# Attention with a gated, routed feed-forward: VectorE's side jobs placed at another point of the block

## The chip, the cores and the metric

The kernel runs on one core of a Trainium2 chip. The metric is the device time of one launch in microseconds (us). Times are medians of several runs; one further execution was taken by the hardware profiler, and its trace is what the profile shows. Engines: PE is TensorE (matmuls), DVE is VectorE, ACT is ScalarE, POOL is GpSimd, SP is SyncE, which here only issues DMAs. Each engine works through its own instructions strictly in the order in which they are written; across engines only semaphores order them.

## What is computed

Cut to what matters (2048 tokens of width 640, 32 heads of width 192, the last 512 rows of the key and value caches, feed-forward width 1536):

```python
xn = layernorm(x)                                  # [2048, 640]
q  = xn @ wq                                       # 32 heads x 192
p  = softmax(q @ k.T * 192**-0.5)                  # per head, 512 keys
s  = concat(p @ v) @ wo                            # [2048, 640]
r   = xn @ w_r                                     # one number per token
idx = the 2 tokens with the largest r              # the routed rows
y   = (silu(xn[idx] @ w_gate) * (xn[idx] @ w_up)) @ w_down * sigmoid(r[idx])
b   = xn with y added to the 2 rows idx
out = x + s * silu(b)
```

Nearly all work is the attention `s`. The routed feed-forward touches two rows only, but needs `r` of all 2048 tokens, a search for the two largest, a gather of these two rows, their own layernorm, and three small matrix products.

## The kernel before

The whole order of work is written out by hand; no scheduler changes it.

**Blocks.** Work goes in 128 numbered blocks. A block b handles, for one pair of heads, 256 query tokens as two halves a = 0, 1 of 128 tokens; two blocks (even, odd) make a step of 512 tokens, 16 blocks a group of four heads over all tokens. From block 12 to block 125 each block emits the tokens of the string `BLOCK = "A S0 M0 W m E0 B S1 M1 P E1 l"`:

- A and B (L340): the two halves of the query projection of the next step on PE, ten matmuls each. In even blocks they have 512 columns, in odd blocks 256, so A and B are long in even blocks and short in odd ones. B is told to wait for the row maximum before it. After B, ACT moves the result to `qT` (L352).
- S0, S1 (L367): scores of one half, six matmuls into one of two PSUM buffers. M0, M1 (L372): DVE's row maximum of these scores, `nm`. E0, E1 (L377): ACT's exponentials, which need `nm`; after E1, SP issues the DMA that transposes them (`pT`, L383).
- W (L447): output projection `wo` of an item six blocks back, 24 matmuls into two PSUM banks; DVE adds both to the accumulator `s_acc` (L468, L470). In this text that is "wo's eviction".
- P: the product with V for block b-2 (L406), 32 matmuls, the second half of them after everything in the list `bg[b]`. Then DVE takes two reciprocals (`rl`, L413), ACT scales one PSUM bank in two instructions (`o_sb`, L420) and DVE the other (`o_sb`, L417): "P V's eviction". SP transposes `o_sb` by DMA (L423). The PSUM banks of P and W come from one pool of two, so W of the next block needs the banks that P V's eviction clears.
- m and l are the two side places: lists of small jobs, by block number.

**Side jobs.** `mid[b]` runs at m, so on DVE behind wo's eviction and ahead of M1. `bg[b]` runs inside P, so on DVE behind M1 and ahead of `rl`. `loads[b]` runs at l, at the end of the block, and holds DMA issues of SP and ACT and copies of POOL: `wo_double` (L151) copies a loaded piece of `wo` to the other 64 partitions, `k_order` (L121) permutes a loaded piece of K. POOL starts these copies when the load has landed.

The routed rows' jobs on DVE: `m_r(n)` (L648, blocks 12 to 27, one each) multiplies a tile of 128 tokens of `xn` by `w_r` and sums; `m_round`, `m_rows` (28) turn the sums; `m_top` (29) finds the two best of each tile, and POOL issues two DMAs that write them to DRAM and read them back to all partitions (L681, L683); `m_sel` (32, m) and `m_tok` (32, inside P) choose the two tokens; `m_own` (33) makes the indices, and POOL issues the gather of the two rows (L717); `m_gather` gives seven pieces (36 to 39, in turn at m and inside P): the mask `oh` (L734), statistics (L186), Newton steps for the root in four pieces (L207 to L222), and the normalised rows `xsel` (L751); `m_ffn(fb)` (blocks 41, 49, 57, inside P) does the gate and up products, ACT's tanh (L772) and two DVE products (L773, L774), and in the block behind turns the result on PE (L778); `m_sig` (60, inside P) makes the sigmoid. From block 71 POOL adds `y` to each tile (L828, L831, L832), and from block 76 on, in every even block at m, DVE forms the gate of one tile (L841); the change leaves these as they are.

Of the kernel before, what the change touches and what calls it, by code (L numbers as in the profile page):

```python
# [13 lines left out]
BF16 = mybir.dt.bfloat16  # L14
# [7 lines left out]
def kernel(ctx, tc, A_x, A_k_cache, A_v_cache, A_wq, A_wo, B_x, B_w_r, B_w_gate, B_w_up, B_w_down, out):  # L22
    nc = tc.nc
    P = 128
# [7 lines left out]
    NTB = S // P  # L32
# [41 lines left out]
    def f_tile(shape, dtype, name, kind="q"):  # L74
        return banks[kind].tile(shape, dtype, name=name, tag="f")
# [107 lines left out]
    def ln_stats(src, mv_ap, parts=P):  # L183
        stats = small.tile([P, nsub, nc.vector.BN_STATS_DIM], FP32, name="stats")
        for c in range(nsub):
            nc.vector.bn_stats(out=stats[0:parts, c, :], in_=src[:, c * sub:(c + 1) * sub])  # L186
        nc.vector.bn_aggr(out=mv_ap, in_=stats[0:parts])
# [8 lines left out]
    def ln_nmr(mean_ap, rstd_ap, nmr_ap):  # L196
        nc.vector.scalar_tensor_tensor(out=nmr_ap, in0=mean_ap, scalar=-1.0, in1=rstd_ap, op0=ALU.mult, op1=ALU.mult)

    def rsqrt_newton(var_ap, out_ap, parts, n):

        T = {}

        def one():
            T["v"] = small.tile([P, 4], FP32, name="nw_v")[0:parts, 0:n]
            T["a"] = small.tile([P, 4], FP32, name="nw_a")[0:parts, 0:n]
            T["i"] = small.tile([P, 4], I32, name="nw_i")[0:parts, 0:n]
            nc.vector.tensor_scalar(out=T["v"], in0=var_ap, scalar1=EPS, scalar2=None, op0=ALU.add)  # L207

        def two():
            nc.vector.tensor_scalar(out=T["i"], in0=T["v"].bitcast(I32), scalar1=1, scalar2=None, op0=ALU.arith_shift_right)  # L210

        def three():
            nc.vector.tensor_scalar(out=out_ap.bitcast(I32), in0=T["i"], scalar1=-1.0, scalar2=float(0x5f3759df), op0=ALU.mult, op1=ALU.add)

        def s1():
            nc.vector.scalar_tensor_tensor(out=T["a"], in0=out_ap, scalar=-0.5, in1=out_ap, op0=ALU.mult, op1=ALU.mult)

        def s2():
            nc.vector.tensor_tensor(out=T["a"], in0=T["a"], in1=T["v"], op=ALU.mult)

        def s3():
            nc.vector.scalar_tensor_tensor(out=out_ap, in0=T["a"], scalar=1.5, in1=out_ap, op0=ALU.add, op1=ALU.mult)  # L222
        return [one, two, three] + [s1, s2, s3] * 3
# [256 lines left out]

    bg = defaultdict(list)
    mid = defaultdict(list)
    loads = defaultdict(list)

    def ln_parts(t5):
# [35 lines left out]
    copies = {"a": nc.scalar.copy, "v": nc.vector.tensor_copy}  # L521

    def flush(k):
        for f in mid.pop(k, []) + loads.pop(k, []) + bg.pop(k, []):
            f()

    def first(token):
# [96 lines left out]
    M = {}  # L624
# [20 lines left out]
    def m_r(n):  # L645
        def f():
            junk = M["s"].tile([P, D], BF16, name="junk", tag="t1")
            nc.vector.scalar_tensor_tensor(out=junk, in0=xn[:, n, :], scalar=1.0, in1=M["wr"], op0=ALU.mult, op1=ALU.mult,  # L648
                                           accum_out=M["r"][:, n:n + 1])
        return f  # L650
# [70 lines left out]
    def m_ffn_piece(fb, q):  # L721
        def f():
            if q == 0:
                M["wgu"] = M["w"].tile([P, 2, DC, 512], BF16, name="wgu", tag="w")
            w, dc = divmod(q, DC)
            src = (B_w_gate, B_w_up)[w].rearrange("(c p) f -> p c f", p=P)
            nc.scalar.dma_start(out=M["wgu"][:, w, dc, :], in_=src[:, dc, fb * 512:(fb + 1) * 512])
        return f

    def m_gather():  # L730

        def mask():
            for j in range(2):
                nc.vector.tensor_scalar(out=M["oh"][:, :, j], in0=M["iota"], scalar1=M["best"][:, 1, j:j + 1], scalar2=0.5,  # L734
                                        op0=ALU.is_equal, op1=ALU.mult)

        def begin():
            M["mv2"] = M["s"].tile([2, 2], FP32, name="mv2")
            M["rs2"] = M["s"].tile([2, 2], FP32, name="rs2")
            ln_stats(M["xg"], M["mv2"], parts=2)  # L740
            M["nw"] = rsqrt_newton(M["mv2"][:, 1:2], M["rs2"][:, 0:1], 2, 1)

        def newton(q):
            for f in M["nw"][3 * q:3 * q + 3]:
                f()

        def apply():
            mv2, rs2 = M["mv2"], M["rs2"]
            ln_nmr(mv2[:, 0:1], rs2[:, 0:1], rs2[:, 1:2])
            M["xsel"] = M["s"].tile([2, D], BF16, name="xsel", tag="t3")  # L750
            nc.vector.tensor_scalar(out=M["xsel"], in0=M["xg"], scalar1=rs2[:, 0:1], scalar2=rs2[:, 1:2], op0=ALU.mult, op1=ALU.add)  # L751
        return [mask, begin] + [lambda q=q: newton(q) for q in range(4)] + [apply]
# [8 lines left out]
    def m_ffn(fb):  # L761

        def mul():
            gu = f_tile([P, 2, P], FP32, "gu_ps")
            for dc in range(DC):
                for c in range(4):
                    nc.tensor.matmul(gu[32 * c:32 * c + 32], lhsT=M["xsT"][:, dc, :], rhs=M["wgu"][:, :, dc, c * P:(c + 1) * P],
                                     start=(dc == 0), stop=(dc == DC - 1), skip_group_check=True)
            th = M["s"].tile([P, 3, P], FP32, name="th", tag="t2")
            M["h"] = M["s"].tile([P, P], BF16, name="h")  # L770
            nc.vector.tensor_copy(out=th[:, 0:2], in_=gu)
            nc.scalar.activation(out=th[:, 2], in_=th[:, 0], func=ACT.Tanh, scale=0.5)  # L772
            nc.vector.scalar_tensor_tensor(out=th[:, 2], in0=th[:, 2], scalar=1.0, in1=th[:, 0], op0=ALU.add, op1=ALU.mult)  # L773
            nc.vector.scalar_tensor_tensor(out=M["h"], in0=th[:, 2], scalar=0.5, in1=th[:, 1], op0=ALU.mult, op1=ALU.mult)  # L774

        def turn():
            h_ps = f_tile([P, P], BF16, "h_ps")
            nc.tensor.transpose(out=h_ps, in_=M["h"], identity=ident)  # L778
            nc.vector.tensor_copy(out=M["hT"][:, fb * 4:(fb + 1) * 4, :].rearrange("p c t -> p (c t)"), in_=h_ps)
        return mul, turn  # L780

    def m_wd_piece(h, q):
        def f():
            if q == 0:
                M["wd"] = M["w"].tile([P, FC, HD], BF16, name="wd", tag="w")
            nc.scalar.dma_start(out=M["wd"][:, 2 * q:2 * q + 2, :],
                              in_=B_w_down.rearrange("(c p) d -> p c d", p=P)[:, 2 * q:2 * q + 2, h * HD:(h + 1) * HD])
        return f
# [53 lines left out]
        return a, b  # L842

    bg[11].append(m_open)
    for n in range(NTB):
        mid[12 + n].append(m_r(n))
    mid[28].append(m_round)
    bg[28].append(m_rows)
    mid[29].append(m_top)
    mid[32].append(m_sel)  # L850
    bg[32].append(m_tok)
    mid[33].append(m_own)
    for q, it in enumerate(m_gather()):
        (mid, bg)[q % 2][36 + q // 2].append(it)
    bg[40].append(m_xsT)
    pieces = {0: (33, (2, 2, 2, 1, 2, 1)), 1: (42, (2, 2, 2, 2, 2)), 2: (49, (2, 2, 2, 1, 2, 1))}
    for fb, km in enumerate((41, 49, 57)):
        k0, counts = pieces[fb]
        at = [k0 + h for h, n in enumerate(counts) for _ in range(n)]
        for q, a in enumerate(at):  # L860
            loads[a].append(m_ffn_piece(fb, q))
        mul, turn = m_ffn(fb)
        bg[km].append(mul)
        bg[km + 1].append(turn)
    for h in range(2):
        for q, a in enumerate((57, 58, 58, 59, 59, 60)):
            loads[a + 5 * h].append(m_wd_piece(h, q))
    bg[60].append(m_sig)
    bg[62].append(m_down(0))
    bg[68].append(m_down(1))  # L870
    bg[69].append(m_sum)
    for n in range(NTB):
        bg[71 + 2 * n].append(m_add(n))
        a, b = m_gate(n)
# [34 lines left out]
    for b in range(HEAD, NB - 2):  # L909
        for token in BLOCK:  # L910
            if token in "AB":
                if b // 2 + 1 < NS:
                    q_phase(b // 2 + 1, ((0, 1), (2,))[b % 2], "AB".index(token))
            elif token[0] == "S":
                scores(b, int(token[1]))
            elif token[0] == "M":
                row_max(b, int(token[1]))
            elif token[0] == "E":
                exps(b, int(token[1]))
            elif token == "W":  # L920
                w_item(b - LAG)
            elif token == "P":
                def between():
                    for f in bg.pop(b, []):
                        f()
                o_item(b - 2, "va", between)
            else:
                for f in {"m": mid, "l": loads}[token].pop(b, []):
                    f()

    def last(token):
# [27 lines left out]
    """.split()  # L959
    for token in LAST:  # L960
        last(token)
    assert not bg and not mid and not loads


# [28 lines left out]
```

## Time and profile before

| what | value |
|---|---|
| median of 3 runs | 808.72 us (808.2 to 810.61) |
| the profiled execution | 807.77 us, span in the trace 806.0 us |
| PE busy | 783.0 us, 97% of the span |
| DVE, ACT, POOL busy | 591.0, 529.3, 310.1 us |
| granted TensorE clock | 1.0 |
| `m_r` on DVE (L648) | 16 instructions, 17.5 us |
| copies of POOL (L151; L121) | 32, 59.3 us; 30, 25.1 us |

A timeline row gives the start in the span, the duration, engine, line, operation, out<-in with shapes, how many instructions were merged into it, and in brackets the idle time of the engine before it with the instruction that ended it. PE's matmuls overlap in the pipeline, so a PE row that starts late need not show all of the lateness as idle time.

### The profile page before, as it was taken

What the parts mean: (1) busy time and instruction counts of PE and PEld (TensorE: products, weight loads), DVE (VectorE), ACT (ScalarE), POOL (GpSimd) and SP (SyncE); (2) the same over time, 40 slices, a digit from 0 to 9 for tenths busy, and PEclk for the clock granted to TensorE, in tenths of its full rate; (3) what the DMA queues carried; (4) which work ended last, traced back from release to release, by engine and by line L of the source; (5) the groups of instructions that cost most, each with busy time, mean ns of one, the idle gap of its engine ahead of it and who ended that gap; (6) DMA issues with size and microseconds to landing.
All of it is one profiled execution on the core that took longest, in us unless ns stands there. A gap on an engine that the chain in (4) does not pass through costs nothing.

```text
span 806.0 us, 26621 instructions
## 1 busy us (share of the span) xinstructions
PE 783.0 (97%) x11354; PEld 579.1 (72%) x11354; DVE 591.0 (73%) x1086; ACT 529.3 (66%) x964; POOL 310.1 (38%) x244
## 2 busy tenths in 40 slices
PE   8799899999999999999999999999999999999997
PEld 4366577777777777777777777777777777777775
DVE  7686588778778667777666667777777777767775
ACT  5677566665666666666666667677776776666662
POOL 1312120011110100101011699959997412564865
PEclk9999999999999999999999999999999999999999
DMA  7998998798999999999998999989898899999992
GB/s 193 188 175 161 199 169 154 152 189 143 191 199 160 181 208 200 196 188 191 200 211 159 171 192 166 182 137 184 173 186 149 153 190 163 209 190 163 178 181 84
DMA packets 445111, 142.29 MB, mean 177 GB/s; under 512 B 412228, under 2 KB 444488, under 8 KB 444992
## 3 DMA queue, kind: packets, MB, share of 16 engines
q1 hardware_dynamic: 435216, 131.18, 93.1%
q10 hardware_dynamic: 8816, 6.88, 3.3%
q0 software_dynamic: 960, 2.52, 1.0%
q8 instruction: 89, 1.46, 0.8%
q14 instruction: 30, 0.25, 0.1%
HBM read 39.98 MB, written 2.62 MB: 53 GB/s over the span
## 4 chain that ended last, share of the span: by engine, by line
PE 85%; DVE 5%; DMA 4%; ACT 3%; issue 2%; POOL 0%; SPq 0%; ACTq 0%; DVEq 0%; POOLq 0%
PE w L447 24%; PE q_ps L340 21%; PE o_ps L406 18%; PE s L367 18%; DVE nm L372 2%; DMA pT<-pexp 2%; PE q_ps L309 2%; ACT o_sb L420 1%; ACT pexp L377 1%; PE warm_ps L163 1%; DMA xnT<-xn 1%; DMA oT<-o_sb 1%; DMA wo_g<-in_A_wo_dram 1%; DMA v_sb<-in_A_v_cache_dram 0%; ACT qT L315 0%
## 5 line engine op out<-in xcount | busy, mean ns | idle before, releaser
L372 DVE TENSOR_REDUCE nm<-s 128x2 f32<-128x1024 f32 x256 | 313.0, 1223 | 135.6 <-PE s L367 131.0
L377 ACT ACTIVATE pexp<-s,nm 128x512 bf16<-128x512 f32 x512 | 323.3, 688 | 90.3 <-DVE nm L372 53.9
L447 PE MATMUL w<-wo_g,oT 64*128 64x320 bf16 x3072 | 231.1, 296 | 4.8 <-ACT o_sb L420 4.5
L340 PE MATMUL q_ps<-xnT,wq_g 64*128 64x512 bf16 (+1 forms) x2340 | 232.4, 323 | 3.2 <-DMA xnT<-xn 1.5
L447 PEld LDWEIGHTS <-oT 64*128 64x128 bf16 x3072 | 171.8, 94 | 62.9 <-issue 7.5
L367 PE MATMUL s<-kT,qT 64*128 64x512 bf16 x1536 | 211.7, 376 | 5.0 <-ACT pexp L377 3.9
L406 PEld LDWEIGHTS <-pT 64*128 64x128 bf16 x4096 | 179.1, 94 | 27.9 <-issue 2.0
L406 PE MATMUL o_ps<-v_sb,pT 64*128 64x193 bf16 x4096 | 197.2, 243 | 0.0
L420 ACT ACTIVATE o_sb<-o_ps,rl 128x192 bf16<-128x192 f32 x256 | 93.6, 417 | 145.7 <-DVE rl L413 140.6
L340 PEld LDWEIGHTS <-wq_g 64*128 64x128 bf16 x2340 | 127.4, 99 | 48.3 <-issue 2.6
L151 POOL COPY wo_g<-wo_g 64x1920 bf16<-64x1920 bf16 x32 | 59.3, 1858 | 222.3 <-DMA wo_g<-in_A_wo_dram 202.1
L367 PEld LDWEIGHTS <-qT 64*128 64x128 bf16 x1536 | 85.4, 94 | 59.8 <-issue 6.4
L470 DVE TENSOR_TENSOR s_acc<-s_acc,w 128x320 f32<-128x320 f32 x192 | 85.0, 484 | 35.4 <-PE w L447 35.4
L352 ACT ACTIVATE qT<-q_ps 128x1024 bf16<-128x1024 f32 x114 | 92.4, 810 | 7.7 <-PE q_ps L340 2.8
L121 POOL COPY k_perm<-k_raw 128x768 bf16<-128x768 bf16 x30 | 25.1, 854 | 143.3 <-DMA k_raw<-in_A_k_cache_dram 111.9
L417 DVE TENSOR_TENSOR o_sb<-o_ps,rl 128x384 bf16<-128x384 f32 x128 | 71.4, 558 | 4.6 <-DVE rl L413 0.2
L831 POOL TENSOR_SCALAR yh<-y_bc,oh 128x640 bf16<-128x640 bf16 x32 | 61.7, 1929 | 3.3 <-DMA y_bc<-y_d 1.7
L832 POOL TENSOR_TENSOR xn<-xn,yh 128x640 bf16<-128x640 bf16 x32 | 44.6, 1395 | 2.7
L413 DVE RECIPROCAL rl<-o_ps 128x2 f32<-128x2 f32 x256 | 30.0, 159 | 14.4 <-PE o_ps L406 8.2
L894 POOL TENSOR_TENSOR s_acc<-s_acc,x_fin 128x640 f32<-128x640 f32 x16 | 22.4, 1397 | 31.3 <-DMA x_fin<-in_A_x_dram 30.8
L828 POOL TENSOR_SCALAR xn<-xn 128x640 bf16<-128x640 bf16 x16 | 29.4, 1838 | 0.8
L478 POOL TENSOR_TENSOR fin_o<-fin_t,s_acc 128x640 bf16<-128x640 f32 x12 | 18.5, 1540 | 17.7 <-DVE fin_t L473 11.1
(138 smaller groups left out, 262.4 us busy)
## 6 DMA issues: line engine op xcount, KB each, us to landing
wo_g<-in_A_wo_dram SPq DMA_DIRECT2D x32, 240.0 KB, 4.3
k_raw<-in_A_k_cache_dram SPq DMA_DIRECT2D x32, 192.0 KB, 3.6
v_sb<-in_A_v_cache_dram SPq DMA_DIRECT2D x32, 192.0 KB, 4.3
wq_g<-in_A_wq_dram SPq DMA_DIRECT2D x14, 288.0 KB, 4.1
wq_g<-in_A_wq_dram SPq DMA_DIRECT2D x14, 192.0 KB, 3.7
x_fin<-in_A_x_dram SPq DMA_DIRECT2D x16, 160.0 KB, 3.6
pT<-pexp SPq DMA_TRANSPOSE x130, 4.9
oT<-o_sb SPq DMA_TRANSPOSE x126, 3.4
```

The source lines that it names most:

```text
L151: nc.gpsimd.tensor_copy(out=grp[g][("wo", pr)][half(1), cs, :], in_=grp[g][("wo", pr)][half(0), cs, :])
L340: mm = nc.tensor.matmul(q_ps[k][:, 0:n] if type(q_ps) is list else q_ps[:, k, 0:n], lhsT=wq[half(r), dc, c:2 * Dh:3], rhs=xnT[half(r), tok ...
L352: nc.scalar.activation(out=out, in_=q_ps[:, :, 0:n], func=ACT.Copy, scale=scale)
L367: nc.tensor.matmul(s_of[b, a][:, r, :], lhsT=qT_of[i][half(r), c, u * P:(u + 1) * P], rhs=grp[g][("kT", pr)][half(r), :, c, :], start=(c = ...
L372: rm = nc.vector.tensor_reduce(out=nm_of[b, a], in_=s_of[b, a], axis=AX.X, op=ALU.max, negate=True)
L377: nc.scalar.activation(out=p_ring[:, b % 2, a, :, hh, :].rearrange("p (x j) e -> p x j e", x=2), in_=s_of[b, a][:, hh, :].rearrange("p (j ...
L406: nc.tensor.matmul(o_of[b][r][:, a, 0:Dh + 1], lhsT=pT_ring[half(r), b % RP, a, k, :], rhs=v_ring[half(r), (g * PAIRS + pr) % RV, k, 0:Dh ...
L417: nc.vector.tensor_tensor(out=o_sb, in0=src, in1=rl[:, r].unsqueeze(2).unsqueeze(3).to_broadcast([P, 2, 3, HK]), op=ALU.mult)
L420: nc.scalar.activation(out=o_sb[:, a], in_=src[:, a], func=ACT.Copy, scale=rl[:, r, a:a + 1])
L447: nc.tensor.matmul(w_ps[r][:, 0:HD], lhsT=oT_ring[half(r), bs[pr] % RT, c, :], rhs=grp[g][("wo", pr)][half(r), c, cs], start=(pr == 0 and ...
L470: nc.vector.tensor_tensor(out=acc, in0=acc, in1=src, op=ALU.add)
L831: nc.gpsimd.tensor_scalar(out=yh, in0=M["y_bc"][:, j, :], scalar1=M["oh"][:, n, j:j + 1], scalar2=None, op0=ALU.mult)
```

## The change

A third list, `end[b]`, runs at l ahead of `loads[b]`: on DVE behind P V's eviction, and so ahead of M0 of the next block. A helper, `spot(b)`, chooses `mid` for even blocks and `end` for odd ones. `m_r` takes blocks 12 to 23 and 25 to 27 by that rule, and its last piece goes to the end of block 24. `m_top` moves to the end of 29, `m_sel` to the end of 31, `m_tok` to m of 32, `m_own` to the end of 33, and the seven pieces of `m_gather` to blocks 34 to 40, one each. The two DVE products of `m_ffn` become a job of their own, `act`, at m of the even block behind; ACT's tanh stays. `m_sig` moves from inside P to m of block 60. Nothing is added or removed: on PE, POOL and SP the order of the instructions is the same as before, on ACT only the tanh of `m_sig` comes ahead of that block's E0.

```diff
+    end = defaultdict(list)
...
-        for f in mid.pop(k, []) + loads.pop(k, []) + bg.pop(k, []):
+        for f in mid.pop(k, []) + loads.pop(k, []) + bg.pop(k, []) + end.pop(k, []):
...
             th = M["s"].tile([P, 3, P], FP32, name="th", tag="t2")
-            M["h"] = M["s"].tile([P, P], BF16, name="h")
             nc.vector.tensor_copy(out=th[:, 0:2], in_=gu)
             nc.scalar.activation(out=th[:, 2], in_=th[:, 0], func=ACT.Tanh, scale=0.5)
+            M["th"] = th
+
+        def act():
+            th = M["th"]
+            M["h"] = M["s"].tile([P, P], BF16, name="h")
             nc.vector.scalar_tensor_tensor(out=th[:, 2], in0=th[:, 2], scalar=1.0, in1=th[:, 0], op0=ALU.add, op1=ALU.mult)
             nc.vector.scalar_tensor_tensor(out=M["h"], in0=th[:, 2], scalar=0.5, in1=th[:, 1], op0=ALU.mult, op1=ALU.mult)
...
-    for n in range(NTB):
-        mid[12 + n].append(m_r(n))
+
+    def spot(b):
+        return (mid, end)[b % 2][b]
+    for n, b in enumerate([*range(12, 24), 25, 26, 27]):
+        spot(b).append(m_r(n))
+    end[24].append(m_r(15))
     mid[28].append(m_round)
     bg[28].append(m_rows)
-    mid[29].append(m_top)
-    mid[32].append(m_sel)
-    bg[32].append(m_tok)
-    mid[33].append(m_own)
-    for q, it in enumerate(m_gather()):
-        (mid, bg)[q % 2][36 + q // 2].append(it)
+    for b, it in enumerate((m_top, None, m_sel, m_tok, m_own, *m_gather())):
+        if it is not None:
+            spot(29 + b).append(it)
...
-        mul, turn = m_ffn(fb)
+        mul, act, turn = m_ffn(fb)
         bg[km].append(mul)
+        mid[km + 1].append(act)
         bg[km + 1].append(turn)
...
-    bg[60].append(m_sig)
+    mid[60].append(m_sig)
...
-                for f in {"m": mid, "l": loads}[token].pop(b, []):
+                for f in mid.pop(b, []) if token == "m" else end.pop(b, []) + loads.pop(b, []):
                     f()
```

More of the change, by code (lines that the diff above doesn't have):

```diff
@@ L779, in turn @@
             nc.vector.tensor_copy(out=M["hT"][:, fb * 4:(fb + 1) * 4, :].rearrange("p c t -> p (c t)"), in_=h_ps)
-        return mul, turn
+        return mul, act, turn
     def m_wd_piece(h, q):
@@ L961 @@
         last(token)
-    assert not bg and not mid and not loads
+    assert not bg and not mid and not end and not loads
 _INS = ['A_x', 'A_k_cache', 'A_v_cache', 'A_wq', 'A_wo', 'B_x', 'B_w_r', 'B_w_gate', 'B_w_up', 'B_w_down']
```

## The prediction, on record before the changed kernel ran

> **What bounds the kernel now.** First the page's head: PE is busy for 783 of 806 us, so the end is set by PE's stream, and a change is worth what it takes from or adds to PE's waits, nothing else.
>
> ```profile
> span 806.0 us, 26621 instructions
> PE 783.0 (97%) x11354; PEld 579.1 (72%) x11354; DVE 591.0 (73%) x1086; ACT 529.3 (66%) x964; POOL 310.1 (38%) x244
> ```
>
> Next the timelines of DVE, PE and ACT over two blocks without side jobs, even block 46 (M0 at 301.15) and odd block 47 (M0 at 307.05).
>
> ```profile
> 301.15 1.23 DVE L372 TENSOR_REDUCE nm<-s 128x2 f32<-128x1024 f32 x1 [0.97 <-PE s L367]
> ...
> 304.50 1.23 DVE L372 TENSOR_REDUCE nm<-s 128x2 f32<-128x1024 f32 x1 [0.93 <-PE s L367]
> 305.79 0.24 DVE L413 RECIPROCAL rl<-o_ps 128x2 f32<-128x2 f32 x2
> ...
> 307.05 1.23 DVE L372 TENSOR_REDUCE nm<-s 128x2 f32<-128x1024 f32 x1 [0.43 <-PE s L367]
> ...
> 309.88 1.23 DVE L372 TENSOR_REDUCE nm<-s 128x2 f32<-128x1024 f32 x1 [0.40 <-PE s L367]
> 311.16 0.24 DVE L413 RECIPROCAL rl<-o_ps 128x2 f32<-128x2 f32 x2
> 311.43 0.56 DVE L417 TENSOR_TENSOR o_sb<-o_ps,rl 128x384 bf16<-128x384 f32 x1
> ```
>
> ```profile
> 312.67 1.81 PE L447 MATMUL w<-wo_g,oT 64*128 64x320 bf16 x24
> 314.30 1.26 PE L340 MATMUL q_ps<-xnT,wq_g 64*128 64x512 bf16 x10
> ...
> 318.58 0.70 PE L447 MATMUL w<-wo_g,oT 64*128 64x320 bf16 x7
> ```
>
> ```profile
> 311.36 0.73 ACT L420 ACTIVATE o_sb<-o_ps,rl 128x192 bf16<-128x192 f32 x2 [1.31 <-DVE rl L413]
> ```
>
> ```profile
> 317.79 0.73 ACT L420 ACTIVATE o_sb<-o_ps,rl 128x192 bf16<-128x192 f32 x2 [0.95 <-DVE rl L413]
> ```
>
> A block lasts 5.90 us (307.05 - 301.15). DVE waits at four places, and these waits are the room for side jobs: ahead of M1 0.93 in even blocks and 0.40 in odd ones; ahead of the next block's M0 0.97 behind an odd block and 0.43 behind an even one. Past that room, lateness costs PE at two points. A late `rl` makes ACT's `o_sb` late, and W of the next block waits for its bank: ACT ends at 312.09 with W at 312.67 behind odd block 47, but at 318.52 with W at 318.58 behind even block 48. Taking 0.05 for the handover, an odd block forgives 0.53 us and an even one nothing. A late M0 holds B: M0 of 312.95 in the same rhythm ends at 314.18, B starts at 314.30; about 0.06 is forgiven.
>
> Then PE's rows that begin with a wait in the changed stretch, and what DVE and POOL did before one of them (block 17).
>
> ```profile
> 105.96 1.81 PE L447 MATMUL w<-wo_g,oT 64*128 64x320 bf16 x24 [0.87 <-ACT o_sb L420]
> 130.54 1.81 PE L447 MATMUL w<-wo_g,oT 64*128 64x320 bf16 x24 [0.79 <-ACT o_sb L420]
> 190.95 1.81 PE L447 MATMUL w<-wo_g,oT 64*128 64x320 bf16 x24 [1.02 <-ACT o_sb L420]
> ...
> 245.78 1.81 PE L447 MATMUL w<-wo_g,oT 64*128 64x320 bf16 x24 [0.65 <-ACT o_sb L420]
> 325.60 1.81 PE L447 MATMUL w<-wo_g,oT 64*128 64x320 bf16 x24 [0.19 <-ACT o_sb L420]
> ...
> 607.31 1.81 PE L447 MATMUL w<-wo_g,oT 64*128 64x320 bf16 x24 [0.60 <-ACT o_sb L420]
> ```
>
> ```profile
> 123.95 1.23 DVE L372 TENSOR_REDUCE nm<-s 128x2 f32<-128x1024 f32 x1 [0.43 <-PE s L367]
> ...
> 126.30 2.19 DVE L648 SCALAR_TENSOR_TENSOR junk<-xn,wr_bc 128x640 bf16<-128x640 bf16 x1
> ...
> 128.43 1.21 DVE L372 TENSOR_REDUCE nm<-s 128x2 f32<-128x1024 f32 x1
> 129.56 0.22 DVE L413 RECIPROCAL rl<-o_ps 128x2 f32<-128x2 f32 x2
> ```
>
> ```profile
> 126.04 1.78 POOL L151 COPY wo_g<-wo_g 64x1920 bf16<-64x1920 bf16 x1 [9.08 <-DMA wo_g<-in_A_wo_dram]
> ```
>
> ```profile
> L648 DVE SCALAR_TENSOR_TENSOR junk<-xn,wr_bc 128x640 bf16<-128x640 bf16 x16 | 17.5, 1096 | 0.2 <-DMA wr_bc<-in_B_w_r_dram 0.2
> ```
>
> So the stalls have one picture: `m_r` met a copy of POOL that had begun 0.26 earlier, stood until the copy's end at 127.82, and took 2.19 instead of some 0.8. The group's mean of 1096 ns over 16 says that about three of them were caught (16 x (1.096 - 0.8) = 4.7 us, some three times 1.5); the waits at 105.96, 130.54 and 190.95 are the three.
>
> **Part by part.** The change moves DVE's jobs; PE, POOL and SP keep their order. The costs of the jobs in one window view (stretch, length, busy PE, PEld, DVE, ...): one free `m_r`, `m_top`, `m_sel`, `m_tok`, one Newton piece, `m_sig`.
>
> ```profile
> 139.07:139.81 0.74, 0.74 (x18) 0.64 (x16) 0.74 (x2) 0.66 (x2) 0.00 (x0) 1.00 0.43 88
> 199.88:200.97 1.09, 1.09 (x26) 0.99 (x24) 0.95 (x7) 0.67 (x2) 0.00 (x0) 1.00 0.34 64
> 217.74:218.65 0.91, 0.91 (x15) 0.55 (x11) 0.88 (x8) 0.79 (x2) 0.00 (x0) 1.00 1.27 286
> 219.90:220.37 0.47, 0.47 (x14) 0.47 (x11) 0.43 (x6) 0.00 (x0) 0.00 (x0) 1.00 1.15 221
> 256.46:256.89 0.43, 0.43 (x13) 0.43 (x10) 0.36 (x5) 0.00 (x0) 0.00 (x0) 1.00 1.14 215
> ...
> 390.76:391.22 0.46, 0.46 (x13) 0.46 (x10) 0.39 (x4) 0.00 (x0) 0.00 (x0) 1.00 0.08 9
> ```
>
> *Removed: `m_r` ahead of M1 in odd blocks.* Free, it needs 0.74 against 0.40 of room: `rl` 0.34 late, under the 0.53 forgiven, so it costs nothing today and its move gains nothing. Caught, block 17: `rl` at 129.56 - 123.95 = 5.61 behind M0 instead of 311.16 - 307.05 = 4.11, so 1.50 late, less 0.53 = 0.97 for PE, of which 0.79 is shown as wait. I add the same 0.18 to the other two: 1.05 + 0.97 + 1.20 = 3.2 us. In the new place (the end, about 4.9 behind M0) a copy like that of block 17, running from 2.09 to 3.87 behind M0, is over a microsecond earlier.
>
> *Removed: jobs inside P.* There DVE's `rl` is due 1.29 behind M1 (305.79 - 304.50); with a job it comes 1.13 (129.56 - 128.43) plus the job. In even blocks that is 1:1 for PE: `m_tok` 1.13 + 0.47 - 1.29 = 0.31, the Newton piece of block 38 0.27, `m_sig` 0.30. The statistics of block 36 cost the wait at 245.78, 0.65 + 0.18 = 0.83. `act` of block 49, with the wait for tanh ahead of it, 0.19 + 0.18 = 0.37; blocks 41 and 57 some 0.05. Sum 2.1. In their new places all of them have at least 0.93 of room.
>
> *Added, by room.* `m_r` at the end of odd blocks 0.74 against 0.97: nothing, as PE is then busy with the long A and S0, for which M0 waits anyhow; were that cover gone, 0.7 each for eight blocks, some 6 us. `m_r(15)` at the end of even block 24: 0.74 - 0.43 - 0.06 = 0.25. `m_top` 1.09 - 0.97 - 0.06 = 0.06. `m_own`, statistics, Newton pieces, mask, `xsel`, `act`, `m_sig`: each under its room; the tanh that goes ahead of E0 stands in ACT's wait for M0. Behind a late end job stands M0, behind it E0 and B.
>
> *Added, waits for DMAs.* `m_sel` comes two blocks behind `m_top` instead of three.
>
> ```profile
> cand_bc<-c_d POOLq DMA_DIRECT2D x1, 32.0 KB, 5.0
> ...
> c_d<-cand POOLq DMA_DIRECT2D x1, 0.2 KB, 3.0
> ```
>
> Two blocks are 11.8 us less 1.1 for `m_top`; the two transfers need 8.0 and about 1 of issuing: 1.6 left, so no wait, but nothing queued behind `m_sel` (M0 first) would be spared if they were 2 us slower. The gather keeps two blocks; nothing of it is near.
>
> *Added, copies of POOL at the new places.* Moved jobs meet other copies:
>
> ```profile
> 212.94 1.78 POOL L151 COPY wo_g<-wo_g 64x1920 bf16<-64x1920 bf16 x1 [7.44 <-DMA wo_g<-in_A_wo_dram]
> ...
> 241.62 0.82 POOL L121 COPY k_perm<-k_raw 128x768 bf16<-128x768 bf16 x1 [13.90 <-DMA k_raw<-in_A_k_cache_dram]
> ...
> 266.54 1.78 POOL L151 COPY wo_g<-wo_g 64x1920 bf16<-64x1920 bf16 x1 [19.43 <-DMA wo_g<-in_A_wo_dram]
> ```
>
> ```profile
> 209.33 1.23 DVE L372 TENSOR_REDUCE nm<-s 128x2 f32<-128x1024 f32 x1 [0.43 <-PE s L367]
> ...
> 264.04 1.23 DVE L372 TENSOR_REDUCE nm<-s 128x2 f32<-128x1024 f32 x1 [0.97 <-PE s L367]
> ```
>
> ```profile
> 241.68 0.93 DVE L734 TENSOR_SCALAR oh<-iota,best 128x16 f32<-128x16 f32 x2
> ```
>
> `m_sel` would start about 4.9 behind M0 of block 31, at 214.2, inside the copy that ends at 214.72. Does a small copy from SBUF to SBUF stand still for POOL? The nearest row is the mask `oh`, small and with one tensor read: the pair began 0.06 behind POOL's copy and took 0.93, to just past the copy's end at 242.44, while `m_tok`'s two instructions over as many columns take 0.47. I take it that `m_sel` stands too: 0.5 + 0.91 - 0.97 - 0.06 = 0.38 (bounds: 0, and 0.8 if the copy comes 0.4 later). The Trainium skill, page "SBUF — State Buffer", section "Who interferes with whom", speaks here against the change: VectorE and GpSimd share one pair of SBUF ports, an instruction of VectorE with two SBUF inputs, or a copy in a two-port mode, waits for the whole of a GpSimd instruction that reads SBUF, and the order of issue decides who blocks. By it `m_sel` stands and every moved job is a new lottery with POOL; without it the 0.38 would fall away. The row of 126.30 agrees.
>
> *Sum.* 3.2 + 2.1 = 5.3 gained; 0.25 + 0.06 + 0.38 = 0.7 lost; 0.4 I keep for small meetings that can't be placed (below): **4.2 us**. The profiled execution took 807.77 (span 806.0 and 1.8 around it): 803.6. Against the median of 808.72, which lies 0.95 above it, that is **804.5**.
>
> **The rivals.**
>
> *A new meeting that costs most of a stall.* The copy at 266.54 falls 2.50 behind M0 of block 40 (264.04), just where `xsel` would now begin, at m (jobs there start 2.3 to 2.4 behind M0: 126.30 - 123.95). If POOL is first, `xsel` stands to 268.32, when M1, due 304.50 - 301.15 = 3.35 behind M0 at 267.39, is already 0.9 late; with some 0.5 for `xsel` itself (the Newton piece has 0.43) that is 1.4, and an even block forgives nothing. If DVE is first, POOL waits and nobody minds. The Newton piece of block 36 with the copy at 241.62 is the same for 0.2. Today's lateness of block 39 goes, so the copy should come later against the grid; I give POOL's win 20%. Result 4.2 + 0.4 - 1.4 = 3.2 down to 1.5 with a second meeting: 805.5 to 807.2.
>
> *Given back later.* With fewer pauses of PE the transposes have less time to catch up; E0 waits for one now and then, and each late one costs 0.2 to 0.5. Or the three caught `m_r` are an accident of the profiled run and the medians hold fewer. For it: who is first is decided by tenths. Against it: the medians are longer, not shorter, than the profiled run. Result a gain of 0 to 2.4: 806.3 to 808.7, chance 13%.
>
> *Slower: the later gates.* From block 76 on, 16 gates (L841) stand ahead of M1 in even blocks while POOL works without pause. One was caught at block 96 and made the wait of 0.60 at 607.31, with the unseen part 0.78. All before it now comes 4 us sooner, and if POOL's chain, which starts when its own DMAs land, slides against the blocks, other gates are caught. To end above before, over five more of the 16 must be caught in full; POOL's start hangs on PE's matmul of block 68, so it should move along with the blocks. At eight more: 4.2 - 6.2 = 2.0 worse, 810.7. Chance 7%.
>
> *It doesn't do what it says:* the instruction order is fixed by hand, so the jobs do stand where the text puts them; no chance of its own.
>
> **How the numbers follow.** Forecast 60% (its own range: 5.3 gained to 3.3, 803.4 to 805.4), new meeting 20%, given back 13%, slower 7%. What this kernel's measurement can tell from no change is about 0.3%, 2.4 us. Faster by more: 60 + 17 of the 20 (gain over 2.4) = 77%. Within: 3 + 13 = 16%. Slower: 7%. For eight in ten the range takes the forecast, the new meeting and a little of the third: 803.0 to 807.3, the low end widened by 0.4 for the spread of the medians.
>
> **What would show it.** PE's waits of 0.87, 0.79 and 1.02 ahead of W in blocks 14, 18 and 28 are gone, and that of 0.65 ahead of W in block 37; L648's mean falls from 1096 to some 820 ns; M0 behind odd blocks of the stretch 13 to 27 waits some 0.2 instead of 0.85 to 0.97; a pair of blocks there lasts 11.8. Wrong would be: `m_r` still at 2 us in some block; B waiting for M0 in blocks 26, 32 or others (the room of 0.97 is then not there); `xsel` at over 1 us in block 40; a wait of DVE for `cand_bc`; or all stalls gone and the time unchanged, which would mean that something other than PE's waits sets the end.

## The result, and the profile after

The changed kernel takes 803.19 us (median of 9 runs, 802.36 to 806.1) against 809.36 us (9 runs, 806.06 to 811.2) for the kernel before on the same chip: a ratio of 0.9933, with a 95% interval of 0.9915 to 0.9951. Its profiled execution took 802.92 us. So it is faster, by 6.2 us by these medians, by 4.0 to 6.9 by the interval of the ratio, and by 4.85 us by the two profiled executions. The forecast's gain of 4.2 lies inside the interval, near its low end, and the median of 803.19 lies 0.2 above the low end of the range of 803.0 to 807.3.

The head of the page of the changed kernel:

```profile
span 801.1 us, 26624 instructions
PE 781.1 (97%) x11354; PEld 576.6 (72%) x11354; DVE 589.8 (74%) x1086; ACT 530.3 (66%) x964; POOL 309.1 (39%) x244
```

PE still sets the end; the span is 4.9 us shorter while PE's work is the same 11354 matmuls. What PE waited for, first before, then after (in total, times, longest):

```profile
PE w L447 <- ACT o_sb L420: 4.5, 8, 1.0
```

```profile
PE w L447 <- ACT o_sb L420: 0.8, 2, 0.6
...
PE xsT_ps L758 <- DVE xsel L752: 0.5, 1, 0.5
```

Six of the eight waits ahead of W are gone, among them the three long ones; the 0.6 that is left is the gate of block 96, caught again. Two new waits stand in their place: the one for `xsel`, and one of 0.2 ahead of the turn of `m_rows` in block 28. The group of `m_r` (now L649):

```profile
L649 DVE SCALAR_TENSOR_TENSOR junk<-xn,wr_bc 128x640 bf16<-128x640 bf16 x16 | 13.4, 835 | 0.8 <-DMA wr_bc<-in_B_w_r_dram 0.8
```

The mean fell from 1096 to 835 ns: no `m_r` stands for a whole copy any more. One still met the end of a copy (block 25, 1.10). Block 17 on DVE, after, the block that the prediction took as its picture:

```profile
122.75 1.23 DVE L372 TENSOR_REDUCE nm<-s 128x2 f32<-128x1024 f32 x1 [0.43 <-PE s L367]
...
126.86 0.24 DVE L413 RECIPROCAL rl<-o_ps 128x2 f32<-128x2 f32 x2
...
127.61 0.82 DVE L649 SCALAR_TENSOR_TENSOR junk<-xn,wr_bc 128x640 bf16<-128x640 bf16 x1
...
128.66 1.23 DVE L372 TENSOR_REDUCE nm<-s 128x2 f32<-128x1024 f32 x1 [0.23 <-PE s L367]
```

`rl` comes 4.11 behind M0 (126.86 - 122.75) instead of 5.61; `m_r` stands behind the eviction, 4.86 behind M0, and M0 of block 18 still waits 0.23 for PE. Block 17 lasts 5.91 (128.66 - 122.75).

**Where the time came from.** M0's rows (DVE L372) mark each block's start, and the difference between neighbours is the block's length. Before, M0 of blocks 12 and 63:

```profile
92.63 1.23 DVE L372 TENSOR_REDUCE nm<-s 128x2 f32<-128x1024 f32 x1 [3.02 <-PE s L367]
...
404.97 1.23 DVE L372 TENSOR_REDUCE nm<-s 128x2 f32<-128x1024 f32 x1 [0.49 <-PE s L367]
```

After:

```profile
92.06 1.23 DVE L372 TENSOR_REDUCE nm<-s 128x2 f32<-128x1024 f32 x1 [3.02 <-PE s L367]
...
400.06 1.22 DVE L372 TENSOR_REDUCE nm<-s 128x2 f32<-128x1024 f32 x1 [0.49 <-PE s L367]
```

The stretch that the change touches fell from 312.34 to 308.00 us, by 4.3; 0.57 had been gained ahead of it, where nothing was changed, so that part of the 4.85 is not the change's. Block lengths from the same rows (a block without jobs lasts 5.90; blocks 29 and 30 differ by 0.05 and -0.04, all others of the stretch agree within 0.02):

| blocks | before | after | gain | forecast |
|---|---|---|---|---|
| 13 + 14 (`m_r` caught) | 6.49 + 6.42 | 5.97 + 5.90 | 1.04 | 1.05 |
| 17 + 18 (`m_r` caught) | 6.35 + 6.42 | 5.91 + 5.90 | 0.96 | 0.97 |
| 27 + 28 (`m_r` caught) | 6.58 + 6.83 | 5.91 + 6.44 | 1.06 | 1.20 |
| 33 (`m_tok`) | 6.23 | 5.91 | 0.32 | 0.31 |
| 36 + 37 (statistics) | 6.20 + 6.42 | 5.90 + 5.91 | 0.81 | 0.83 |
| 39 (Newton piece) | 6.18 | 5.91 | 0.27 | 0.27 |
| 49 + 50 (`act`) | 6.61 + 6.54 | 6.68 + 6.11 | 0.36 | 0.37 |
| 41 + 42, 57 + 58 (`act`) | 25.64 | 25.57 | 0.07 | 0.05 |
| 60 to 62 (`m_sig`) | 18.71 | 18.40 | 0.31 | 0.30 |
| 24 + 25 (`m_r(15)`) | 5.90 + 6.11 | 6.12 + 5.88 | 0.01 | -0.25 |
| 31, 44 (late transposes in before) | 6.07 + 6.21 | 5.90 + 5.90 | 0.48 | none |
| 12 (E0 waits for a transpose) | 6.60 | 7.01 | -0.41 | none |
| 40 (`xsel`) | 6.22 | 7.14 | -0.92 | a rival |

In block 44 of before the profile puts E0's wait of 2.20 down to wo's eviction, which E0 does not read; in x8_changed_again the same wait, 2.23, is put down to a transpose, and I take both for that.

The gains of the first nine rows make 5.2 of the forecast's 5.3. The loss that was not in the forecast's sum is block 40. There, on DVE and POOL, after:

```profile
259.25 1.23 DVE L372 TENSOR_REDUCE nm<-s 128x2 f32<-128x1024 f32 x1 [0.55 <-PE s L367]
...
261.60 1.58 DVE L197 SCALAR_TENSOR_TENSOR rs<-mv,rs 2x1 f32<-2x1 f32 x1
263.21 0.43 DVE L752 TENSOR_SCALAR xsel<-xg,rs 2x640 bf16<-2x640 bf16 x1
263.57 1.21 DVE L372 TENSOR_REDUCE nm<-s 128x2 f32<-128x1024 f32 x1
```

```profile
261.39 1.78 POOL L151 COPY wo_g<-wo_g 64x1920 bf16<-64x1920 bf16 x1 [17.90 <-DMA wo_g<-in_A_wo_dram]
```

POOL's copy begins 2.14 behind M0. The last Newton step `rs`, two numbers, begins 0.21 later and ends with the copy, at 263.18 against 263.17; free it takes 0.14. `xsel` follows, and M1 begins 4.32 behind M0 instead of 3.35.

### The profile page after: what moved, and what is told of

Read it like the earlier page. It is cut to its first block, busy times and chain, and to the rows that moved or that the text cites. A ratio compares the mean times of both kernels' runs of the same rounds, so it can differ in the third digit from the quotient of the medians.

```text
span 801.1 us, 26624 instructions
## 1 busy us (share of the span) xinstructions
PE 781.1 (97%) x11354; PEld 576.6 (72%) x11354; DVE 589.8 (74%) x1086; ACT 530.3 (66%) x964; POOL 309.1 (39%) x244
## 4 chain that ended last, share of the span: by engine, by line
PE 89%; DMA 4%; DVE 3%; ACT 2%; issue 1%; POOL 0%; SPq 0%; DVEq 0%; ACTq 0%; POOLq 0%
PE w L447 24%; PE q_ps L340 22%; PE o_ps L406 20%; PE s L367 19%; DMA pT<-pexp 2%; PE q_ps L309 2%; ACT pexp L377 1%; DVE nm L372 1%; PE warm_ps L163 1%; DMA xnT<-xn 1%; DMA wo_g<-in_A_wo_dram 1%; ACT o_sb L420 0%; ACT qT L315 0%; DVE fin_o L475 0%; ACT qT L352 0%
## 5 line engine op out<-in xcount | busy, mean ns | idle before, releaser
L372 DVE TENSOR_REDUCE nm<-s 128x2 f32<-128x1024 f32 x256 | 313.1, 1224 | 135.0 <-PE s L367 130.7
L352 ACT ACTIVATE qT<-q_ps 128x1024 bf16<-128x1024 f32 x114 | 92.4, 811 | 5.3
L121 POOL COPY k_perm<-k_raw 128x768 bf16<-128x768 bf16 x30 | 25.0, 851 | 139.6 <-DMA k_raw<-in_A_k_cache_dram 108.1
```

The source lines that it names most:

```text
L352: nc.scalar.activation(out=out, in_=q_ps[:, :, 0:n], func=ACT.Copy, scale=scale)
L372: rm = nc.vector.tensor_reduce(out=nm_of[b, a], in_=s_of[b, a], axis=AX.X, op=ALU.max, negate=True)
```

## Experiments

Theory 1: PE's stalls came from jobs that made `rl` late (those of `m_r` by standing behind a copy of POOL), and a job costs its lateness less the room at its place. Rival A: the caught `m_r` are an accident of one trace, so the medians gain less. Rival B: the place counts by itself, the copies don't. Times to M0 are given for two stretches, from block 13 to 29 (`m_r`'s) and from 29 to 63 (the rest): 98.31 and 207.43 us before, 95.24 and 205.74 after. The expectations count the first stretch from block 12, whose own length swings from 6.60 to 7.34 with a wait of E0 for a transpose; counted so, it took 104.91 before, 102.26 after, 101.79 in x1_r_only, 104.40 in x2_rest_only, 103.04 in x3_no_copy and 103.31 in x4_all_end. Timed runs are compared with the kernel before on the same chip.

**x1_r_only: only `m_r` is moved.** The rest keeps its old places; `act` is split off but runs where its two products stood.

```diff
+    for n, b in enumerate([*range(12, 24), 25, 26, 27]):
+        spot(b).append(m_r(n))
+    end[24].append(m_r(15))
...
     mid[29].append(m_top)
     mid[32].append(m_sel)
     bg[32].append(m_tok)
...
         bg[km].append(mul)
+        bg[km].append(act)
```

> Only m_r is moved, as in the change; all later jobs stay in the old places. Theory 1 (PE lost its time to m_r standing behind POOL's copies, and to jobs inside P of even blocks): from M0 of block 12 to M0 of block 29 the stretch takes 102.3 us as in the changed kernel instead of 104.9, from there to block 63 it stays at 207.4 as before; in all 2.6 us faster than before, a ratio of about 0.997. Rival (the gain is the later jobs' or that of transposes that happened to land sooner): under 1 us gained in the first stretch.

Measured: 806.27 us (12 runs) against 808.82 (35 runs), ratio 0.9965 [0.9943, 0.9986]; the stretches took 95.05 and 207.22. In it `m_r`'s group, and PE's waits ahead of W:

```profile
L649 DVE SCALAR_TENSOR_TENSOR junk<-xn,wr_bc 128x640 bf16<-128x640 bf16 x16 | 13.3, 828 | 0.3 <-DMA wr_bc<-in_B_w_r_dram 0.3
```

```profile
PE w L447 <- ACT o_sb L420: 1.6, 4, 0.7
```

The three long waits are gone and the first stretch has the whole gain of 3.3, the second next to none. Blocks 33, 36, 37 and 39 have the lengths of before, block 40 too (6.21).

**x2_rest_only: everything but `m_r` is moved.**

```diff
-    for n, b in enumerate([*range(12, 24), 25, 26, 27]):
-        spot(b).append(m_r(n))
-    end[24].append(m_r(15))
+    for n in range(NTB):
+        mid[12 + n].append(m_r(n))
```

> m_r stays where it was, all later jobs are moved as in the change. Theory 1: one to three m_r of odd blocks still take over 2 us and PE waits 0.8 to 1.0 ahead of the W behind each; from M0 of block 29 to that of block 63 the stretch takes 205.7 as in the changed kernel (with a meeting in block 40) or 204.7 (without) instead of 207.4; in all 1.7 to 2.7 us faster than before, ratio 0.997 to 0.998. Rival: the later stretch gains under 0.7.

Measured: 806.42 us (12 runs), ratio 0.9974 [0.9956, 0.9993]; stretches 97.24 and 205.85. The two halves of the change add up: x1_r_only's first stretch (3.26 gained) and this one's second (1.58) make 4.84, against 4.76 in the changed kernel. The ratios, 2.8 and 2.1 us, agree, but their intervals are about 1.7 us wide to each side. `m_r`'s group in it:

```profile
L649 DVE SCALAR_TENSOR_TENSOR junk<-xn,wr_bc 128x640 bf16<-128x640 bf16 x16 | 16.0, 1001 | 1.0 <-DMA wr_bc<-in_B_w_r_dram 1.0
```

Two of the three `m_r` were caught again (blocks 17 and 27, which last 6.35 and 6.55, where before had 6.35 and 6.58); the one in block 13 slipped through, because the copy came 3.83 behind M0 instead of 2.23. So in this trace rival A holds for a third of the sum. Block 40 lasted 7.26; its rows on DVE and POOL:

```profile
263.58 0.14 DVE L197 SCALAR_TENSOR_TENSOR rs<-mv,rs 2x1 f32<-2x1 f32 x1
263.75 2.00 DVE L752 TENSOR_SCALAR xsel<-xg,rs 2x640 bf16<-2x640 bf16 x1
```

```profile
263.80 1.78 POOL L151 COPY wo_g<-wo_g 64x1920 bf16<-64x1920 bf16 x1 [17.29 <-DMA wo_g<-in_A_wo_dram]
```

Here `rs` got through and `xsel` stood, though its recorded start is 0.05 ahead of the copy's: a recorded order this close doesn't tell who is first.

**x3_no_copy: the old places, but no copy to meet.** Five pieces of `wo` that POOL copied in blocks 13 to 27 are loaded a second time from DRAM by SP instead.

```diff
+            if (g, c) in ((1, 1), (1, 2), (1, 3), (2, 0), (2, 1)):
+                loads[b0 + at].append(lambda c=c: wo_again(g, c))
+            else:
+                loads[b0 + at + 2].append(lambda c=c: wo_double(g, c))
```

> The kernel before with every job in its old place, but five pieces of wo (those whose copies POOL made in blocks 13 to 27) are loaded a second time by DMA into the other 64 partitions instead of being copied by POOL. Theory 1: m_r ahead of M1 in odd blocks then takes 0.8 everywhere and costs PE nothing (0.34 late, 0.53 forgiven); M0 of block 12 to M0 of block 29 takes some 102.0, about 3 us less than before, unless the added 1.2 MB of loads delay transposes, which I put at up to 1 us back. Rival (the place ahead of M1 in odd blocks costs by itself): the stretch stays near 104.9.

Measured: 808.14 us (12 runs), ratio 0.9996 [0.9975, 1.0017]; stretches 95.73 and 209.06. `m_r`'s group:

```profile
L657 DVE SCALAR_TENSOR_TENSOR junk<-xn,wr_bc 128x640 bf16<-128x640 bf16 x16 | 13.1, 816 | 1.4 <-DMA wr_bc<-in_B_w_r_dram 1.4
```

No `m_r` is caught, and the first stretch gains 2.6 of the 3.1 with every job in its old place. That settles rival B: at m a free `m_r` costs nothing, and the copies were the price. But the whole kernel gains nothing; block 12 lasts 7.31, block 44 6.49, block 48 6.83. ACT's row of block 48:

```profile
314.65 1.26 ACT L383 ACTIVATE pexp<-s,nm 128x512 bf16<-128x512 f32 x2 [2.83 <-DMA pT<-pexp]
```

E0 there waits 2.83 us for a transpose of the exponentials. Whether the five loads delay such transposes, or this trace only had bad luck, one profile can't say, since other kernels show single waits of the kind too; that the median is some 2 us above x1_r_only speaks for the loads. It stays open.

**x4_all_end: every `m_r` behind P V's eviction, in even blocks too.** This prices the even end, which the prediction put at 0.25.

```diff
-    for n, b in enumerate([*range(12, 24), 25, 26, 27]):
-        spot(b).append(m_r(n))
-    end[24].append(m_r(15))
+    for n in range(NTB):
+        end[12 + n].append(m_r(n))
```

> The changed kernel with all sixteen m_r at the end of their blocks, so that seven even blocks more have one ahead of the odd block's M0. Theory 1 with the rooms of the prediction: each of these is 0.74 against 0.43 + 0.06, so B of the odd block behind starts 0.25 later; M0 of block 12 to M0 of block 29 takes 102.3 + 7 x 0.25 = 104.0, and the whole is 1.7 slower than the changed kernel, ratio to before about 0.995. Rival (only the meetings with POOL matter): same as the changed kernel, 102.3 and 0.993.

Measured: 805.69 us (12 runs), ratio 0.9966 [0.9946, 0.9985]; stretches 95.97 and 207.16. The end of block 20 and block 21 on DVE:

```profile
146.49 0.81 DVE L649 SCALAR_TENSOR_TENSOR junk<-xn,wr_bc 128x640 bf16<-128x640 bf16 x1
...
147.23 1.22 DVE L372 TENSOR_REDUCE nm<-s 128x2 f32<-128x1024 f32 x1
...
153.06 1.23 DVE L372 TENSOR_REDUCE nm<-s 128x2 f32<-128x1024 f32 x1 [0.23 <-PE s L367]
```

M0 of block 21 doesn't wait for PE, it is late; the even block lasts 6.12 and the odd one behind it 5.83 (153.06 - 147.23), and so in all seven pairs from 14 to 27. Together that is 11.95 instead of 11.80: 0.15 each, since 0.07 of the 0.22 is caught up in the odd block. So the rival (only the meetings count) is out, and the price is 0.15 instead of the 0.25 expected. In the second stretch block 60 lasted 7.09, with E0 waiting 2.84 for a transpose, and block 40 7.31 with `xsel` at 2049 ns.

**x6_no_copy_40: the changed kernel without the copy in block 40.** The piece of `wo` that POOL copies there is loaded twice instead.

```diff
+            if (g, c) == (3, 0):
+                loads[b0 + at].append(lambda c=c: wo_again(g, c))
+            else:
+                loads[b0 + at + 2].append(lambda c=c: wo_double(g, c))
```

> The changed kernel, but the one piece of wo whose copy POOL makes in block 40 is loaded a second time by DMA instead. If the normalised rows of the gather (rs, xsel) stood behind that copy, rs and xsel take 0.14 and 0.43 and block 40 lasts 6.2 instead of 7.14: 0.9 us sooner at block 63, apart from what one added load of 240 KB does to transposes. Rival (xsel is late in its new place whatever POOL does, by the waits behind the Newton steps): block 40 stays at 7.1.

Measured: 804.65 us (4 runs), ratio 0.9936 [0.991, 0.9961]. Block 40 on DVE:

```profile
258.92 1.23 DVE L378 TENSOR_REDUCE nm<-s 128x2 f32<-128x1024 f32 x1 [0.55 <-PE s L373]
...
261.26 0.14 DVE L203 SCALAR_TENSOR_TENSOR rs<-mv,rs 2x1 f32<-2x1 f32 x1
261.44 0.43 DVE L761 TENSOR_SCALAR xsel<-xg,rs 2x640 bf16<-2x640 bf16 x1
...
265.13 1.23 DVE L378 TENSOR_REDUCE nm<-s 128x2 f32<-128x1024 f32 x1 [0.43 <-PE s L373]
```

Nothing else was changed, and the block lasts 6.21 instead of 7.14: the copy was the cause. The stretch from 29 to 63 still took 206.26, because blocks 41, 49 and 58 lasted 7.12, 6.87 and 6.90 instead of 6.67, 6.68 and 6.11; in block 41 E0 waited 1.13 for a transpose again. Whether the added load did that isn't shown, and by the medians the kernel can't be told from the changed one.

**x7_sel_in_P: `m_sel` inside P of block 31, one run.** This asks whether small copies from SBUF to SBUF stand behind POOL, on which the 0.38 for `m_sel` rested, and whether the room of an odd block is 0.53.

```diff
-            spot(29 + b).append(it)
+            (bg[31] if it is m_sel else spot(29 + b)).append(it)
```

> The changed kernel with m_sel inside P of block 31, where POOL's copy of wo should be running (it ran from 3.06 to 4.84 behind M0 of that block; m_sel would begin about 4.0 behind it). If small copies from SBUF to SBUF stand for POOL as the prediction took it, val takes 0.9 or more, rl is 1.6 late and blocks 31 and 32 together last about 12.9. If they don't stand, val takes 0.17, rl is 0.75 late, 0.53 is forgiven, and the two blocks last 12.0.

Measured: 805.25 us in one run, block 31 5.91 and block 32 6.42. Its rows on DVE, POOL and PE:

```profile
206.69 1.23 DVE L372 TENSOR_REDUCE nm<-s 128x2 f32<-128x1024 f32 x1 [0.43 <-PE s L367]
...
210.66 0.55 DVE L690 COPY val<-cand_bc 128x32 f32<-128x32 f32 x1
...
211.85 0.23 DVE L413 RECIPROCAL rl<-o_ps 128x2 f32<-128x2 f32 x2
```

```profile
209.39 1.78 POOL L151 COPY wo_g<-wo_g 64x1920 bf16<-64x1920 bf16 x1 [4.66 <-DMA wo_g<-in_A_wo_dram]
```

```profile
212.83 1.81 PE L447 MATMUL w<-wo_g,oT 64*128 64x320 bf16 x24 [0.35 <-ACT o_sb L420]
```

The first copy takes 0.55 instead of 0.17 and ends with POOL's, at 211.21 and 211.17: small copies stand too. `rl` is 5.16 behind M0 instead of 4.11, 1.05 late; less the room of 0.53 that makes 0.52, and block 32 is 0.52 too long, of which 0.35 shows as PE's wait and 0.17 doesn't. The two blocks last 12.33, between the 12.9 and the 12.0 expected, because the copy came 2.70 behind M0 instead of 3.06 and less of it was left.

**x5_better and x9_packed: the gather packed closer, so that it is through before block 40.** `xsel` then stands at m of block 38. x9_packed has the changed kernel's places of `m_r`; x5_better also moves `m_r` one block later (blocks 13 to 28, with none at an even end).

```diff
+    G = m_gather()
+    for b, its in ((29, [m_top]), (31, [m_sel]), (32, [m_tok]), (33, [m_own]), (34, G[:1]), (35, G[1:2]), (36, G[2:4]), (37, G[4:6]), (38, G[6:])):
+        spot(b).extend(its)
```

> The changed kernel with m_r in blocks 13 to 28 (none at the end of an even block, none in block 12, where it waits for w_r) and the gather's pieces packed into the end of 35, m of 36, the end of 37 and m of 38, so that block 40 has none. Theory 1: rooms are 0.91 of 0.93, 0.86 of 0.97 and 0.54 of 0.93; the waits in blocks 24 and 40 go, 0.15 and 0.9 us, and block 12 may save up to 0.5: 1.0 to 1.6 us faster than the changed kernel, ratio to before 0.991 to 0.992. Rival (each new place meets another copy): no gain on the changed kernel.

> The changed kernel with m_r in its places (one still at the end of block 24) and only the gather's seven pieces packed as in the version before: the statistics at the end of 35, two Newton pieces at m of 36, two at the end of 37, xsel at m of 38, so that nothing stands in block 40 where POOL copies. Theory 1: block 40 lasts 6.22 instead of 7.12, blocks 36 to 38 stay at 5.9; M0 of block 13 to M0 of block 63 takes 300.1 instead of 301.0, and the whole is 0.9 faster than the changed kernel, unless transposes that land late take it back. Rival (pieces packed two to a place overrun their rooms or meet POOL's copy in block 36): blocks 36 to 38 lose what block 40 gains.

Measured: x5_better 803.47 us (6 runs), ratio 0.9929 [0.9907, 0.9952], stretches 95.57 and 205.46; x9_packed 803.26 us (6 runs) against 807.26 (11 runs), ratio 0.9942 [0.9919, 0.9965], stretches 95.06 and 205.05. `xsel` in x9_packed, M0 of block 40 and M1 there, and the copy that now meets nothing:

```profile
250.26 0.43 DVE L752 TENSOR_SCALAR xsel<-xg,rs 2x640 bf16<-2x640 bf16 x1
...
259.54 1.23 DVE L372 TENSOR_REDUCE nm<-s 128x2 f32<-128x1024 f32 x1 [0.96 <-PE s L367]
...
262.89 1.23 DVE L372 TENSOR_REDUCE nm<-s 128x2 f32<-128x1024 f32 x1 [0.93 <-PE s L367]
```

```profile
261.78 1.78 POOL L151 COPY wo_g<-wo_g 64x1920 bf16<-64x1920 bf16 x1 [18.11 <-DMA wo_g<-in_A_wo_dram]
```

M1 is back at 3.35 behind M0, block 40 lasts 6.22, and blocks 13 to 62 take 300.12 against 300.98 in the changed kernel: the stretch has lost the meeting. By the medians neither kernel can be told from the changed one; the intervals are wider than the 0.9 at stake. In x5_better the `m_r` at the end of block 25 (1.40 us) met another copy, L121, and its block lasted 6.25. That place is the changed kernel's too, where the same meeting took 1.10 and the block 5.88, so it isn't the move's fault.

**x8_changed_again: the changed kernel once more, unedited,** for the scatter from run to run.

> The changed kernel itself, beside the three others on one chip. Theory 1: rs or xsel of block 40 stands behind POOL's copy again (block 40 at 7.1 to 7.3) and no m_r of blocks 13 to 27 takes over 1.2; M0 of block 12 to M0 of block 63 within 0.7 of 308.0. Rival (the meeting in block 40 was an accident of one run): block 40 at 6.2.

Measured: 804.45 us (12 runs, 802.39 to 807.25) against 808.93 (17 runs), ratio 0.9945 [0.9927, 0.9962]; stretches 95.06 and 206.03. Block 40 lasted 7.12, with `xsel` at 1864 ns; no `m_r` took over 1.2 (the longest, in block 13, 1.19). All blocks of the table from 13 to 42 that hold a moved job repeat within 0.15; what differs are single late transposes (block 44 at 6.24).

## Why the prediction was right, step by step

- **The picture of the stalls** (a late `rl`, made late by a job or by a copy of POOL): shown. Moving the jobs (x1_r_only, x2_rest_only) and removing the copies (x3_no_copy) each take the stalls away. The three terms of `m_r`, 3.2 in sum, measured 3.06; the third is 1.20 where block 28 lasts 6.30, as in x1_r_only.
- **The jobs inside P**, 2.1 by "1:1 for PE": measured 2.1, each within 0.02. That an instruction's length can be added to `rl`'s time one for one is borne out.
- **The rooms**: the 0.53 that an odd block forgives came back as 0.53 in x7_sel_in_P, and the 0.74 of a free `m_r` fits the room of 0.97 behind odd blocks. But the new place is not as free of copies as the block-17 argument has it: in block 13 the copy came 3.48 to 3.93 behind M0 in five kernels and lengthened `m_r` there to between 1.02 and 1.47; the longest, in x7_sel_in_P, made block 13 last 6.32 instead of 5.97.
- **`m_r(15)` at an even end**, 0.25: mis-sized. M0's lateness is 0.22, and the odd block behind recovers 0.07, which the step left out: 0.15. Block 25 got shorter by 0.23 for a reason outside the forecast. In before, x2_rest_only and x3_no_copy M1 of block 24 stands 3.71 behind M0 instead of 3.36, held until ACT's `qT` is done ([0.54 <-ACT qT L352] in before); `rl` comes 4.85 instead of 4.64 behind M0, and block 25 lasts 6.11 to 6.18. In the changed kernel that wait is gone. Why M1 waits for `qT` there isn't shown; x5_better, which also has an `m_r` at m of block 24, doesn't have the wait.
- **`m_top`**, 0.06: nothing in sum (block 29 is 0.05 longer, block 30 0.04 shorter).
- **`m_sel` behind a copy**, 0.38: the step's mechanism holds (x7_sel_in_P), its timing doesn't. In the changed kernel the copy comes 3.06 behind M0 instead of 3.61, and `m_sel` starts 0.01 after it has ended:

```profile
206.13 1.22 DVE L372 TENSOR_REDUCE nm<-s 128x2 f32<-128x1024 f32 x1 [0.43 <-PE s L367]
...
210.98 0.17 DVE L690 COPY val<-cand_bc 128x32 f32<-128x32 f32 x1
```

```profile
209.19 1.78 POOL L151 COPY wo_g<-wo_g 64x1920 bf16<-64x1920 bf16 x1 [4.89 <-DMA wo_g<-in_A_wo_dram]
```

- **The new meeting in block 40**, a rival at 20%: this step failed. It came, and in the traces of all five kernels that have `xsel` and the copy in that block (copy at 2.14 to 2.61 behind M0, block 7.12 to 7.31). DVE needs 2.35 to 2.95 behind M0 for `rs` and `xsel`, and the copy of 1.78 covers part of that at each of these starts, so the meeting was near certain; the 20% took it for a matter of luck. In three of the five POOL was first by the record; in the other two the copy is recorded 0.05 and 0.09 behind `xsel`, and why `xsel` stood there too isn't shown. The argument that the copy would come later, since block 39's lateness goes, was wrong. SP's rows before and after:

```profile
259.17 1.33 SPq L383 DMA_TRANSPOSE pT<-pexp  x1
260.55 1.99 SPq L115 DMA_DIRECT2D k_raw<-in_A_k_cache_dram  x1
262.59 0.64 SPq L146 DMA_DIRECT2D wo_g<-in_A_wo_dram  x1
```

```profile
254.38 1.33 SPq L383 DMA_TRANSPOSE pT<-pexp  x1
255.76 1.63 SPq L115 DMA_DIRECT2D k_raw<-in_A_k_cache_dram  x1
257.44 0.64 SPq L146 DMA_DIRECT2D wo_g<-in_A_wo_dram  x1
```

  POOL's copy starts 3.95 behind the issue of its load in both (266.54 - 262.59, 261.39 - 257.44), and that issue follows SP's transpose, which lies 4.87 ahead of M0 in both (264.04 - 259.17, 259.25 - 254.38). The grid carries the copy along; it moved 0.36 earlier only because the issue of `k_raw` between them took 1.63 instead of 1.99. The price of 1.4 was too high as well: the meeting cost 0.92 here, where the copy came 0.36 earlier, and 1.04 in x2_rest_only, where `xsel` ended 0.17 behind the copy instead of the 0.5 allowed for it.
- **The sum** came out because errors cancelled, which is luck: 0.25 + 0.06 + 0.38 + 0.4 kept back were 1.1 of loss in the forecast, and 0.15 + 0.92 = 1.1 were lost, in another place. By the table, 5.20 - 0.92 + 0.01 (blocks 24 and 25) + 0.07 (transposes) = 4.36, and the stretch shows 4.34.
- **Given back later**: partly seen, of either sign. The late transposes in blocks 12, 31 and 44 make +0.07 in sum. **The later gates**: no further gate was caught; that of block 96 was, as before.

## What to carry to other kernels

Read the room of each place from the waits of the engine whose lateness counts; lateness less room gave the nine gains in the table to within 0.15 us, block by block. What it missed was a copy's new meeting, and the wait in block 24. When a job moves, look up which of the other engine's long copies cross its new place, and if both hang on the same rhythm, expect their windows to meet again in most runs (block 40 did in five traces of five; block 13, where the copy began anywhere from 1.69 to 3.93 behind M0, did not). What a meeting costs then hangs on which engine is first, and tenths of a microsecond decide that: the five copies of `wo` in blocks 13 to 27 of before all met an `m_r`, three with POOL first, and two with VectorE first, where `m_r` took its free time. And judge edits worth under a microsecond by the blocks they touch, since a single late transfer elsewhere moves the total by as much.

## What the runs showed of the hardware

- A short VectorE instruction can stand as long as a long one: a step on 2x1 numbers (0.14 free) took 1.58 behind a copy of POOL, `xsel` (0.43) 1.86 to 2.05. In x5_better two TENSOR_SCALAR steps on 2x1 numbers (at 238.88 and 239.06) ran in their usual 0.14 during a copy (238.89 to 239.71), while the next step, which reads two such operands, took 0.49 and ended 0.02 behind it.
- The order decides who stands, and it goes both ways. In block 15 of before `m_r` began 0.13 ahead of POOL's copy: it took its free 0.81, and the copy took 2.33 instead of 1.78.

```profile
114.50 0.81 DVE L648 SCALAR_TENSOR_TENSOR junk<-xn,wr_bc 128x640 bf16<-128x640 bf16 x1
```

```profile
114.63 2.33 POOL L151 COPY wo_g<-wo_g 64x1920 bf16<-64x1920 bf16 x1 [11.39 <-DMA wo_g<-in_A_wo_dram]
```

- Not every POOL instruction that reads SBUF holds VectorE up for its whole length. Gates before (L841, 0.82 free) beside POOL's two instructions for each row:

```profile
520.06 1.88 POOL L831 TENSOR_SCALAR yh<-y_bc,oh 128x640 bf16<-128x640 bf16 x1
...
590.69 1.88 POOL L831 TENSOR_SCALAR yh<-y_bc,oh 128x640 bf16<-128x640 bf16 x1
...
603.20 1.40 POOL L832 TENSOR_TENSOR xn<-xn,yh 128x640 bf16<-128x640 bf16 x1
```

```profile
520.63 0.89 DVE L841 SCALAR_TENSOR_TENSOR xn<-tz,xn 128x640 bf16<-128x640 f32 x1
...
591.45 0.82 DVE L841 SCALAR_TENSOR_TENSOR xn<-tz,xn 128x640 bf16<-128x640 f32 x1
603.25 2.02 DVE L841 SCALAR_TENSOR_TENSOR xn<-tz,xn 128x640 bf16<-128x640 f32 x1
```

  A gate that began 0.05 behind L832 took 2.02, to past its end. One that began 0.76 behind L831 took its free 0.82 with 1.12 of L831 still to run; one that began 0.57 behind it took 0.89, and in x1_r_only one that began 0.37 behind it took 1.10. So L831 held VectorE only early in its 1.88, until some 0.6 behind its start. The Trainium skill, page "SBUF — State Buffer", section "Who interferes with whom", has a VectorE instruction with two SBUF inputs contend with a GpSimd instruction that reads SBUF; the copies and L832 agree for their whole length, L831 for its first part alone.
